# A fused dilated-attention and token/channel mixer kernel: a DMA transpose issued from ScalarE's queue, one block through another PSUM bank, two gate sums moved

## The chip, the cores and the metric

The kernel runs on one core of one Trainium2 chip. The metric is the time of one execution in device microseconds; the time before is the median of three runs. A profile of one further execution gives the span from the first to the last instruction, and every instruction's start and duration. TensorE has two rows in it: PE for the matmuls and PEld for the weight loads that overlap them. DVE is VectorE, ACT is ScalarE, POOL is GpSimd, SP is SyncE, which issues most DMAs here. A DMA that is issued from an engine's queue holds that queue while it is issued.

## The reference

Eight batches, eight heads, 576 positions of 64 numbers. Heads 0 to 3 see the last 32 positions, heads 4 to 7 every fourth of the last 128 (the dilated half). The attention's output x (576 x 512 for a batch) goes through a mixer:

```python
scores = (q @ k.T) / sqrt(64)                       # masked: plain window, or dilated
x = softmax(scores) @ v                             # heads side by side: (B, 576, 512)
h = relu(x.T @ w_tok1) @ w_tok2                     # token mixing, 576 -> 256 -> 576
u = x + h.T
out = u + relu(u @ w_ch1) @ w_ch2                   # channel mixing, 512 -> 1536 -> 512
```

## The kernel before

TensorE is given one long hand-made order. `interleave` takes a main sequence, `gen_main(b)` for batch b, and a list of steps with due times; it walks the main sequence, adds up costs that are written beside each piece, and puts a step in where the sum has reached its due time. The times are only numbers that set the order of the instructions; nothing is measured. Below, "block b" is what is issued while `gen_main(b)` runs. In it lie, for batch b, the channel mixing; for batch b+1, the attention's product with v (`values`), the token mixing (`emit_h1`, `emit_u`) and the turning of u; for batch b+2, the casts, the turning of q and k by DMA (`dma_steps`) and the scores with their exponentials (`scores_twin`); for batch b+3, the loads.

**The channel mixing.** `gen_main` makes twelve gate blocks of 128 channels (tile `gp`, L934; the last 64 rows of two batches together in tile `gt`, L925), and ScalarE writes relu of each into the SBUF tensor `gt` (L109). `gen_out` multiplies these by the second weights. It does the 2 x 2 block product with seven products in place of eight, so VectorE first makes sums of gate blocks (`gate_sums`, L737, four kinds named 1 to 4, each in two halves of 0.5 to 1 us) and, once, of weights. Products with the original weights and with `wsum_a`, `wsum_b` are summed in two PSUM banks, px (tile `yx`) and pw (tile `yw`); VectorE adds u and moves them to the SBUF tile `o` (`with_u`, L793; `with_t`, L798), and SP stores `o`. A bank is free for its next product when that add is done. In odd batches `tails` first multiplies the last 64 rows (tile `yp`, L747) and adds u to them (L752).

**u in three forms.** `emit_u` leaves u of a batch in the tile `u`, the dilated half (columns 256 to 511) with its rows sorted by their remainder by four, as attention gave it. The gate blocks need u transposed, the last add needs u with its rows in natural order. From batch 2 on this is done by DMA: SP transposes the whole of u into `utm` (L702) and, for odd batches, its last rows into `utt` (L700); ScalarE copies the dilated half of `utm` into `utd` with the rows in natural order (`uT_place`, L863, two copies); and `u_natural` transposes `utd` back onto the dilated half of u (L708, eight blocks of 128 x 128). There is one `utd`, so the next batch's two copies wait for that transpose, and so do the two `with_u` of the dilated half, (1, 1) and (0, 1). In the batches 0 and 1 TensorE makes the transposes, and VectorE copies them out of a PSUM bank (`emit_uT`).

**Scores to v.** For each half g of the heads, `scores_twin` lets TensorE fill six PSUM banks; ScalarE takes eight (g = 0) or six exponentials from them (L547), GpSimd multiplies the results by the masks (L115, tiles `attp`, `attd` and, for the last rows, `attt`), and only then can `values` of the next block run on TensorE. Heads 4 to 7 need `attd` and the second mask of `attt`.

**Queues and waits.** Each engine's queue runs in the order of issue, and a waiting instruction holds what is behind it. The DMAs that SP and ScalarE issue raise eight semaphores in turn (`DMAHW0` to `DMAHW7`); each waits first for the DMA before it on its own semaphore, so the name in that wait tells which one it raises. PSUM banks are taken in turn from rings: "main" (three banks), "sc" (two) and "fl" (three).

Of the kernel before, what the change touches and what calls it, by code (L numbers as in the profile page):

```python
# [9 lines left out]
FP16 = mybir.dt.float16  # L10
# [4 lines left out]
B = 8  # L15
# [53 lines left out]
def kernel(  # L69
# [11 lines left out]
    nc = tc.nc  # L81
# [583 lines left out]

    def emit_uT(b, cb):
        odd = b % 2
        p = bank("fl" if cb % 2 == (cb > 1 if b else 0) else "main", 3, f"tpu_{b}_{cb}", FP16)
        if odd:
            t = sb.tile([128, 640], FP16, tag="ut1", bufs=4, name=f"uT_{b}_{cb}")  # L670
        else:
            if b not in uT0:
                uT0[b] = sb.tile([128, 4, 512], FP16, tag="ut0", bufs=1, name=f"uT_{b}")
            t = uT0[b][:, cb]
        eng = nc.scalar if cb == 2 and not b else nc.vector
        m0 = 128 * odd
        if cb < 2:
            for s in range(4):
                nc.tensor.transpose(out=p[:, m0 + 128 * s:m0 + 128 * s + 128],
                                    in_=u16(b, s)[:, cb], identity=ident)  # L680
            if odd:
                nc.tensor.transpose(out=p[:, 0:128], in_=u16t[b // 2][:, cb], identity=ident)
            copy(eng, t, p[:, 0:512 + m0])
        else:
            grid = p[:, 0:4 * RS].rearrange("p (r i) -> p r i", i=RS)
            m0 = 32 * odd
            for s in range(4):
                nc.tensor.transpose(out=grid[:, s, m0:m0 + 128], in_=u16(b, s)[:, cb], identity=ident)
            if odd:
                nc.tensor.transpose(out=grid[:, :, 0:32], in_=u16t[b // 2][:, cb], identity=perm)  # L690
            copy(eng, natural(t), grid[:, :, 0:128 + m0].rearrange("p r m -> p m r"))
        uT[(b, cb)] = (t[:, 128:640], t[:, 0:128]) if odd else (t, None)
# [9 lines left out]
            nc.sync.dma_start_transpose(out=uTm[i].rearrange("p x s t -> p (x s) t"),  # L702
                                        in_=u16w[b].rearrange("p x s c -> p (x s c)"))

    def u_natural(b):
        u = u16w[b]
        if turned(b):
            nc.sync.dma_start_transpose(out=u[:, 2:4].rearrange("p x s c -> p (x s) c"),  # L708
                                        in_=uTd.rearrange("p x t -> p (x t)"))
            return  # L710
        for cb in (2, 3):
            nc.sync.dma_start_transpose(out=u[:, cb], in_=uT[(b, cb)][0])
# [26 lines left out]
    def gen_out(b):  # L739
# [16 lines left out]

        base = turn["main"]
        ahead = odd and not last
        gate_sums(b, 1, (2, 1, 4) if ahead else (2,))
        if odd and not last:  # L760
            tail = tails()
            yield next(tail)
            spare.append(base)
            yield from tail
        else:
            spare.append(base)
        turn["main"] = base + 2
# [145 lines left out]
    def gen_main(b):  # L913
        odd = b % 2
        order = CBS if b else range(4)
        m0 = 640 * odd

        def w3_block(cb, mb):
            return w3[mb // 4][:, cb, mb % 4:512:4]

        def gp_tails(g):
            p = bank("main", 3, f"gt_{b}_{g}")
            for i in range(4):
                for cb in order:
                    nc.tensor.matmul(  # L925
                        out=p[:, 128 * i:128 * i + 128], lhsT=w3_block(cb, 4 * g + i), rhs=uT[(b, cb)][1],
                        start=(cb == order[0]), stop=(cb == order[-1]))
            relu(nc.scalar, gta[:, 4 * g:4 * g + 4, 512:640],
                 p.rearrange("p (i t) -> p i t", t=128))

        for mb in range(NMB):
            p = bank("main", 3, f"gp_{b}_{mb}")
            for i, cb in enumerate(order):
                nc.tensor.matmul(out=p, lhsT=w3_block(cb, mb), rhs=uT[(b, cb)][0], start=(i == 0), stop=(i == 3))  # L934
                if i == 1:
                    yield 0.43
            relu(nc.vector if (mb in (1, 3, 5, 6) if b == 0 else mb in (1, 3, 5) if b == 1 else False) else nc.scalar, gta[:, mb, m0:m0 + 512], p)
            yield 0.43
            if odd and mb in (3, 6, 9):
                gp_tails(mb // 3 - 1)  # L940
                yield 0.9
            if b and mb == (6 if b == 1 else 10):
                for g in range(2):
                    gate_sums(b, g, (3,))
            if b and mb == (11 if b == 1 else 10):
                gate_sums(b, 0, (2, 1, 4) if odd and b + 1 < B else (2, 1))
        if b:
            yield from gen_out(b)
            return
        for i in (1, 2, 3):  # L950
            weight_sum(i)
        for s in range(4):
            if s == 2:
                weight_sum(4)
            p = bank("main", 3, f"yp_{b}_{s}")
            o32 = sb.tile([128, DM], FP32, tag="o32", bufs=4, name=f"o32_{b}_{s}")
            for half in range(2):
                c = slice(256 * half, 256 * half + 256)
                for mb in range(NMB):
                    a0 = s if half else 128 * s  # L960
                    nc.tensor.matmul(  # L961
                        out=p[:, c], lhsT=gta[:, mb, a0:512:4] if half else gta[:, mb, a0:a0 + 128],
                        rhs=w4[mb][:, c], start=(mb == 0), stop=(mb == NMB - 1))
                    if mb == 5:
                        yield 0.65
                if half:
                    nc.vector.tensor_tensor(out=blocks4(o32), in0=blocks4(p), in1=u16(b, s), op=ALU.add)
                    for i in range(2):
                        d = slice(256 * i, 256 * i + 256)
                        o = out[b, 0:512, d].rearrange("(m r) c -> r m c", r=4)[s] if i else \  # L970
                            out[b, 128 * s:128 * s + 128, d]
                        nc.sync.dma_start(out=o, in_=o32[:, d])
                yield 0.65
# [193 lines left out]
    for b in range(B):  # L1167
# [15 lines left out]
        elif b == 1:  # L1183
            steps += at(13.5, 0.0, [lambda: u_natural(1)])
            va = value_steps(2, 0.0, 1.0)
            steps += [(0.8 + 0.4 * i, c, f) for i, (_, c, f) in enumerate(scores2[10:])]
            steps += [(t, c, f) for t, (_, c, f) in zip((2.2, 3.0, 4.8, 5.6, 8.2, 9.0, 10.4, 11.2), va)]
            steps += mix_steps(2, 7.0, 13.0, 15.1, 24.6, 1.0, 5.6, 0.8)
            casts = cast_steps(3)
            steps += [(6.0 + 0.5 * i, 0.0, casts[i]) for i in (0, 2, 4, 6, 8)]  # L1190
            steps += [(9.5 + 1.0 * i, 0.0, lambda i=i: cast_qk(3, "q", i, nc.scalar)) for i in range(4)]
            steps += score_steps(3, 21.0, 9.5, lag=0.1)
            steps += at(20.8, 0.9, load_steps(4))
            loads, turns, places = [], dma_steps(3), place_steps(3)

            def some_v(lo, hi):
                if not loads:
                    loads.extend(load_v_steps(3))
                for f in loads[lo:hi]:
                    f()  # L1200

            steps += at(6.0, 0.0, [lambda: some_v(0, 4)]) + at(8.1, 0.0, [turns[0], turns[1], lambda: some_v(4, 7)])
            steps += at(10.6, 0.0, [turns[2], turns[3], lambda: some_v(7, 8)]) + at(12.6, 0.0, [turns[4]])
            steps += at(11.0, 0.3, casts[9:14]) + at(12.5, 0.0, [places[i] for i in (0, 1, 4)])
            steps += at(13.0, 0.3, casts[14:16]) + at(14.0, 0.0, places[2:4]) + at(14.2, 0.0, casts[16:])
        else:
            late = 2.4 * (b % 2)
            steps += at(14.6 + late / 6, 0.0, [lambda b=b: u_natural(b)])
            if b + 1 < B:
                va = value_steps(b + 1, 0.4, 0.95)  # L1210
                steps += va[:6] + [(t + late / 5, c, f) for t, c, f in va[6:]] + mix_steps(
                    b + 1, 5.4 + late / 6, 8.2 + late / 6, 10.6 + late / 6, 22.4 + late, 0.9, 4.1, 1.0)
            if b + 2 < B:
                steps += at(2.0, 0.6, cast_steps(b + 2)) + score_steps(b + 2, 21.4 if b % 2 else 18.0, 8.4 if b % 2 else 6.4)
                places = place_steps(b + 2)
                steps += at(8.5, 0.7, dma_steps(b + 2)) + at(12.0, 0.4, places[:4])
                steps += at(19.6 if b % 2 else 17.2, 0.0, places[4:])
            if b + 3 < B:
                steps += at(17.6, 0.9, load_steps(b + 3))
# [31 lines left out]
```

## Time and profile before

| | us |
|---|---|
| median of 3 runs (lowest to highest) | 278.54 (277.87 to 278.73) |
| the profiled execution, its own time | 278.42 |
| its span, first to last instruction | 276.6 |
| clock granted to TensorE, mean | 1.000 |
| VectorE busy | 168.3 |
| ScalarE busy | 149.0 |
| GpSimd busy | 158.8 |
| the busiest DMA queue (q1), share of the 16 engines in the span | 75.9% |

In a timeline each row has the start and the duration in us, the engine, the line, the operation with its output and inputs, and in square brackets how long the engine stood idle before it and what released it. SPq is SP's queue: its duration is the issue, not the transfer. The transfer's end is given as "DMA to landing", counted from the start of the issue.

### The profile page before, as it was taken

To read this page: it belongs to the slowest core of one execution; us is meant where nothing else is said; L and a number is where in the kernel's file an instruction comes from. 1 tells how busy PE (TensorE), PEld (TensorE's weight loads), DVE (VectorE), ACT (ScalarE), POOL (GpSimd) and SP (SyncE) were. 2 spreads that over 40 slices of the span, in tenths; PEclk is the share of its full clock that TensorE was granted. 3 is DMA by queue.
4 is the path that set the end of the run, shared out by engine and by line. 5 is a ranking of instruction groups with operands and counts; after the bars stand their busy time and mean duration, and the time that the engine had idled before them with its cause. 6 is when DMAs were issued, how large, how long until landed. Compare 5 with 4: busy or idle time off the path is not lost.

```text
span 276.6 us, 6790 instructions
## 1 busy us (share of the span) xinstructions
PE 265.8 (96%) x2694; PEld 197.2 (71%) x2694; DVE 168.3 (61%) x340; ACT 149.0 (54%) x291; POOL 158.8 (57%) x214
## 2 busy tenths in 40 slices
PE   6899999999999999997999999999999999999994
PEld 2796676897666876685775876687776866786673
DVE  6767668575568655674649454775475473961363
ACT  2864774363674465467545656476546565236500
POOL 7880760389858759849973589739980870000000
PEclk9999999999999999999999999999999999999999
DMA  7999999995979799999999999989999220553015
GB/s 216 271 248 238 291 241 210 316 241 159 343 132 226 151 316 281 233 165 259 304 221 186 257 280 255 172 156 316 304 211 148 81 79 2 99 147 78 0 40 152
DMA packets 116783, 55.50 MB, mean 201 GB/s; under 512 B 84976, under 2 KB 115696, under 8 KB 116752
## 3 DMA queue, kind: packets, MB, share of 16 engines
q1 hardware_dynamic: 112096, 49.63, 75.9%
q0 software_dynamic: 2640, 3.94, 7.9%
q10 hardware_dynamic: 2016, 1.51, 1.8%
q8 instruction: 21, 0.34, 0.5%
q14 instruction: 10, 0.08, 0.1%
HBM read 38.12 MB, written 9.44 MB: 172 GB/s over the span
## 4 chain that ended last, share of the span: by engine, by line
PE 85%; DMA 7%; DVE 4%; issue 1%; ACT 1%; ACTq 0%; POOL 0%; DVEq 0%
PE gp L934 29%; PE yx L778 12%; PE yw L778 9%; PE h1p L637 5%; PE up L649 4%; PE gt L925 4%; PE yp L961 4%; PE yp L747 3%; DMA lt<-in_k_dram 3%; PE sc L522 3%; DMA u<-utd 2%; DMA w1p<-in_moe_w_tok_dram 2%; PE h1p L635 1%; PE av L614 1%; PE av L619 1%; DVE gt L737 1%
## 5 line engine op out<-in xcount | busy, mean ns | idle before, releaser
L109 ACT ACTIVATE gt<-gp 128x512 f16<-128x512 f32 x89 | 53.2, 598 | 50.4 <-PE gp L934 50.1
L778 PEld LDWEIGHTS <-gt 128*128 128x128 f16 x600 | 57.0, 98 | 10.2 <-issue 2.0
L934 PE MATMUL gp<-utd,w 128*128 128x512 f16 x144 | 54.7, 380 | 0.0
L934 PE MATMUL gp<-utm,w 128*128 128x512 f16 x144 | 54.6, 379 | 0.0
L934 PEld LDWEIGHTS <-w 128*128 128x128 f16 x384 | 39.1, 113 | 19.8 <-issue 0.5
L115 POOL TENSOR_TENSOR attp<-attp,const 128x1280 f16<-128x1280 f16 x12 | 31.6, 2637 | 23.4 <-ACT attp L547 23.4
L737 DVE TENSOR_TENSOR gt<-gt 128x768 f16<-128x768 f16 x56 | 32.2, 605 | 12.5 <-ACT gt L109 12.2
L115 DVE TENSOR_TENSOR xn<-av,rec 128x320 f16<-128x320 f32 x64 | 31.4, 491 | 2.2
L115 POOL TENSOR_TENSOR attd<-attd,const 128x1024 f16<-128x1024 f16 x12 | 25.5, 2124 | 7.7 <-issue 5.4
L934 PE MATMUL gp<-uT,w 128*128 128x512 f16 x96 | 25.8, 380 | 0.0
L793 DVE TENSOR_TENSOR o<-yx,u 128x512 f32<-128x512 f32 x22 | 15.2, 689 | 11.2 <-PE yx L778 10.5
L778 PE MATMUL yx<-w,gt 128*128 128x256 f16 x168 | 20.6, 273 | 0.0
L778 PE MATMUL yx<-wsum_a,gt 128*128 128x256 f16 x168 | 20.6, 273 | 0.0
L547 ACT ACTIVATE attp<-sc 128x480 f16<-128x480 f32 (+1 forms) x36 | 15.9, 538 | 8.7 <-PE sc L522 8.7
L655 DVE TENSOR_TENSOR u<-up,xn 128x512 f16<-128x512 f32 x26 | 17.8, 688 | 4.1 <-PE up L649 4.1
L626 DVE RECIPROCAL rec<-av 128x5 f32<-128x5 f32 x64 | 12.2, 191 | 12.2 <-PE av L623 12.1
L105 POOL CAST c_k<-l_k 128x512 f16<-128x512 f32 x29 | 17.6, 616 | 2.2 <-DMA l_k<-in_k_dram 1.3
L863 ACT COPY utd<-utm 128x512 f16<-128x512 f16 x12 | 12.7, 1129 | 10.3 <-DMA u<-utd 6.6
L105 POOL CAST c_q<-l_q 128x512 f16<-128x512 f32 x26 | 16.3, 630 | 2.9 <-DMA l_q<-in_q_dram 2.2
L664 DVE TENSOR_TENSOR u16t<-up,xn 64x512 f16<-64x512 f32 x7 | 4.8, 689 | 21.0 <-PE up L660 21.0
L109 ACT ACTIVATE h<-h1p 128x256 f16<-128x256 f32 x31 | 11.8, 384 | 8.9 <-PE h1p L637 8.4
L798 DVE TENSOR_TENSOR o<-yw,o 128x512 f32<-128x512 f32 x13 | 9.0, 691 | 11.4 <-PE yw L778 11.3
(158 smaller groups left out, 549.6 us busy)
## 6 DMA issues: line engine op xcount, KB each, us to landing
l_q<-in_q_dram SPq DMA_DIRECT2D x15, 512.0 KB, 6.6
l_k<-in_k_dram SPq DMA_DIRECT2D x14, 512.0 KB, 7.4
out_dram<-o SPq DMA_DIRECT2D x26, 256.0 KB, 4.1
l_vn<-in_v_dram SPq DMA_DIRECT2D x32, 128.0 KB, 6.7
l_vd<-in_v_dram SPq DMA_DIRECT2D x16, 256.0 KB, 4.2
w<-in_moe_w_ch_dram POOLq DMA_DIRECT2D x6, 512.0 KB, 7.6
out_dram<-o SPq DMA_DIRECT2D x17, 128.0 KB, 2.7
l_vt<-in_v_dram SPq DMA_DIRECT2D x8, 256.0 KB, 4.7
```

Of the source, the lines that this page charges most:

```text
L105: eng.tensor_copy(out=out, in_=in_)
L109: nc.scalar.activation(out=out, in_=in_, func=AF.Relu)
L115: eng.tensor_tensor(out=out, in0=x, in1=y, op=ALU.mult)
L547: nc.scalar.activation(out=out, in_=in_, func=AF.Exp, scale=0.125)
L626: nc.vector.reciprocal(out=rec[:, :, 0], in_=av[:, :, 64])
L637: nc.tensor.matmul(out=p, lhsT=w[:, s, j], rhs=x[:, s, c], start=False, stop=(s == 3))
L655: nc.vector.tensor_tensor(out=u16(b, s), in0=blocks4(p), in1=blocks4(xn[b][:, s]), op=ALU.add)
L737: nc.vector.tensor_tensor(out=out, in0=x, in1=y, op=op)
L778: nc.tensor.matmul(out=p, lhsT=gta[:, k0 + mb, r:r + 128], rhs=weights[:, mb, c], start=(first and not mb and (not a or len(parts) > 2)), ...
L793: nc.vector.tensor_tensor(out=grid(o[(i, j)]), in0=grid(p), in1=u, op=ALU.add)
L863: nc.scalar.copy(out=natural(uTd[:, cb - 2]), in_=uTm[i][:, cb].rearrange("p r m -> p m r"))
L934: nc.tensor.matmul(out=p, lhsT=w3_block(cb, mb), rhs=uT[(b, cb)][0], start=(i == 0), stop=(i == 3))
```

## The change

Three edits. First, `emit_uT` takes one of batch 1's four blocks (cb = 1) through a bank of the ring "fl" in place of "main"; the output products of batch 0 use "main". Second, in odd blocks the gate sum 4 of the second half, and in block 1 that of the first half too, is issued behind the last rows' products and their add, no longer ahead. Third, for the batches 2 to 5 `u_natural` issues its transpose from ScalarE's queue, and at a later place (due time 17.3, or 19.7 in odd blocks, against 14.6 and 15.0); the batches 6 and 7 stay as they were.

```diff
     def emit_uT(b, cb):
-        p = bank("fl" if cb % 2 == (cb > 1 if b else 0) else "main", 3, f"tpu_{b}_{cb}", FP16)
+        p = bank("fl" if (cb != 2 if b else cb % 2 == 0) else "main", 3, f"tpu_{b}_{cb}", FP16)
...
-    def u_natural(b):
+    def u_natural(b, queue=nc.sync):
         u = u16w[b]
         if turned(b):
-            nc.sync.dma_start_transpose(out=u[:, 2:4].rearrange("p x s c -> p (x s) c"),
+            queue.dma_start_transpose(out=u[:, 2:4].rearrange("p x s c -> p (x s) c"),
                                         in_=uTd.rearrange("p x t -> p (x t)"))
...
-        gate_sums(b, 1, (2, 1, 4) if ahead else (2,))
+        gate_sums(b, 1, (2, 1) if ahead else (2,))
         if odd and not last:
             tail = tails()
             yield next(tail)
             spare.append(base)
             yield from tail
+            if b == 1:
+                gate_sums(b, 0, (4,))
+            gate_sums(b, 1, (4,))
...
-                gate_sums(b, 0, (2, 1, 4) if odd and b + 1 < B else (2, 1))
+                gate_sums(b, 0, (2, 1, 4) if odd and 1 < b < B - 1 else (2, 1))
...
-            steps += at(14.6 + late / 6, 0.0, [lambda b=b: u_natural(b)])
+            steps += at(14.6 + late / 6 if b + 2 >= B else 17.3 + late, 0.0,
+                        [lambda b=b: u_natural(b, nc.sync if b + 2 >= B else nc.scalar)])
```

SP's queue in block 2, before, with the waits of each row: the turning of k and q of batch 4 (`tt`, `kr`, `qt`), then `utm` of batch 3, u of batch 2, `utt` of batch 3, then loads.

```order
L353 DMA_TRANSPOSE qt<-c_q_1957 128x8x128 [waits DMAHW2_49]
L702 DMA_TRANSPOSE utm_90<-u_3_2104 128x16x128 [waits DMAHW3_49,DVE_49]
L708 DMA_TRANSPOSE u_2_1643<-utd 128x8x128 [waits DMAHW4_49,Activation_49]
L700 DMA_TRANSPOSE utt<-u16t_95 128x4x128 [waits DMAHW5_49]
L198 DMA lt_2176<-in_q_dram 64x8x64 [waits DMAHW6_49]
```

The same place of SP's queue with the change:

```order
L353 DMA_TRANSPOSE qt<-c_q_1957 128x8x128 [waits DMAHW2_49]
L702 DMA_TRANSPOSE utm_90<-u_3_2104 128x16x128 [waits DMAHW3_49,DVE_49]
L700 DMA_TRANSPOSE utt<-u16t_95 128x4x128 [waits DMAHW4_49]
L198 DMA lt_2176<-in_q_dram 64x8x64 [waits DMAHW6_49]
L198 DMA lt_2176<-in_k_dram 64x8x64 [waits DMAHW7_49]
```

The transpose of u has left SP's queue; `utm` raises semaphore 3, `utt` now 4, and 5 is that of the transpose that went to ScalarE.

ScalarE's queue in block 2, before: the last relu, a copy of k, and the exponentials of batch 4's first half.

```order
L109 ACTIVATE gt<-gp_11_2151 128x512 [waits PE_49]
L103 COPY kt<-kr 128x512 [waits DMAHW7_49,Pool_49]
L547 ACTIVATE attp<-sc_0_5_2193 128x2x128 [waits PE_49,Activation_49,Pool_49]
L547 ACTIVATE attt<-sc_0_5_2193 128x2x64 [waits Activation_49]
L547 ACTIVATE attp<-sc_0_0_2188 128x3x160 [waits Activation_49]
```

The same place with the change:

```order
L109 ACTIVATE gt<-gp_11_2150 128x512 [waits PE_49]
L103 COPY kt<-kr 128x512 [waits DMAHW7_49,Pool_49]
L708 DMA_TRANSPOSE u_2_1643<-utd 128x8x128 [waits DMAHW3_49,DMAHW4_49,DMAHW2_49,DMAHW5_49,DMAHW1_49,DMAHW6_49,DMAHW0_49,Activation_49]
L547 ACTIVATE attp<-sc_0_5_2193 128x2x128 [waits PE_49,Pool_49]
L547 ACTIVATE attt<-sc_0_5_2193 128x2x64
L547 ACTIVATE attp<-sc_0_0_2188 128x3x160
```

The transpose stands ahead of the eight exponentials, and it waits for seven of the DMA semaphores, among them 3 and 4, which `utm` and `utt` raise when they have landed. In the blocks 3, 4 and 5 it stands at the same place; in 3 and 5 there is no `utt`, and it waits for `utm`.

VectorE's queue in block 1, before: six gate sums ahead of the last rows' add (L752).

```order
L655 TENSOR_TENSOR u_2_1643<-up_3_1666,xn_1363 128x4x128
L737 TENSOR_TENSOR gt<-gt 128x3x256 x6
L752 TENSOR_TENSOR o_1_4_1740<-yp_4_1681,u16t_94 128x512
L793 TENSOR_TENSOR o_1_00_1760<-yx_1745,u_1_1040 128x512
L798 TENSOR_TENSOR o_1_00_1760<-yw_1762,o_1_00_1760 128x512
```

And with the change:

```order
L655 TENSOR_TENSOR u_2_1643<-up_3_1666,xn_1363 128x4x128
L737 TENSOR_TENSOR gt<-gt 128x3x256 x4
L752 TENSOR_TENSOR o_1_4_1738<-yp_4_1679,u16t_94 128x512
L737 TENSOR_TENSOR gt<-gt 128x3x256 x2
L796 TENSOR_TENSOR o_1_00_1760<-yx_1745,u_1_1040 128x512
```

Two of the six sums stand behind that add. TensorE's and GpSimd's orders of instructions are the same as before.

## The prediction

> **What bounds the kernel now.** I read the busy times first, then the list of waits, then the timeline of each engine where TensorE stood still.
>
> ```profile
> PE 265.8 (96%) x2694; PEld 197.2 (71%) x2694; DVE 168.3 (61%) x340; ACT 149.0 (54%) x291; POOL 158.8 (57%) x214
> ...
> ACT utd L863 <- DMA u<-utd: 6.6, 2, 4.2
> PE yw L778 <- DVE o L793: 1.5, 1, 1.5
> PE yp L961 <- DVE o L967: 0.4, 1, 0.4
> ```
>
> TensorE is busy for 96% of the span: the time is its work plus the gaps in its row. From 40 us on, its timeline shows only three of 0.2 us or more:
>
> ```profile
> 63.70 0.82 PE L961 MATMUL yp<-w,gt 128*128 128x256 f16 x6 [0.35 <-DVE o L967]
> 92.11 1.47 PE L778 MATMUL yw<-w,gt 128*128 128x256 f16 x12 [0.20 <-DVE o L752]
> 126.18 0.81 PE L778 MATMUL yw<-wsum_b,gt 128*128 128x256 f16 x6 [1.48 <-DVE o L793]
> ```
>
> These are the three places of the change: 0.35 + 0.20 + 1.48 = 2.03 us is all that it can win. What it can lose is not so bounded: TensorE's order is fixed, so any input that is late shifts everything behind it, to the end.
>
> **The two small edits.** At 63.70 TensorE waits for a "main" bank, since batch 1's cb = 1 block holds one turn of that ring; with that block in "fl" the bank before it is free. Worth 0.35 us at most. At 92.11 it waits for the last rows' add, which stood behind six gate sums; two of them behind it free the bank in time. Worth 0.20 us. Neither adds work. But both lie ahead of block 2, where below another chain decides, so I take them as absorbed: 0 of the possible 0.55 us.
>
> **The moved transpose, block 2.** Before, around the third gap:
>
> ```profile
> 117.89 1.09 ACT L103 COPY kt<-kr 128x512 f16<-128x512 f16 x1
> 120.16 0.38 ACT L547 ACTIVATE attp<-sc 128x256 f16<-128x256 f32 x1 [1.19 <-PE sc L522]
> ...
> 122.66 0.35 ACT L547 ACTIVATE attt<-sc 128x128 f16<-128x128 f32 x1
> ...
> 117.41 2.11 SPq L702 DMA_TRANSPOSE utm<-u  x1
> 119.61 1.69 SPq L708 DMA_TRANSPOSE u<-utd  x1
> 121.35 1.71 SPq L700 DMA_TRANSPOSE utt<-u16t  x1
> ...
> 125.44 0.69 DVE L793 TENSOR_TENSOR o<-yw,u 128x512 f32<-128x512 f32 x1 [2.16 <-DMA u<-utd]
> ```
>
> The times to landing of the three transposes, in the rows of each line (the six of L708 and of L702 together, then L702 and L700 here, then L702 in block 4):
>
> ```profile
> L708 SPq DMA_TRANSPOSE u<-utd x6: 1261/1554/1992, 119.6 to 249.0; - x6
> DMA to landing us min/median/max: 3.2/3.8/5.7
> ...
> L702 SPq DMA_TRANSPOSE utm<-u x6: 1317/2006/2934, 90.6 to 237.6; - x6
> DMA to landing us min/median/max: 4.3/4.6/6.3
> ...
> L702 SPq DMA_TRANSPOSE utm<-u x1: 2108/2108/2108, 117.4 to 117.4; - x1
> DMA to landing us min/median/max: 6.3/6.3/6.3
> ...
> L700 SPq DMA_TRANSPOSE utt<-u16t x1: 1714/1714/1714, 121.3 to 121.3; - x1
> DMA to landing us min/median/max: 4.6/4.6/4.6
> ...
> L702 SPq DMA_TRANSPOSE utm<-u x1: 1317/1317/1317, 177.8 to 177.8; - x1
> DMA to landing us min/median/max: 4.3/4.3/4.3
> ```
>
> So `utm` landed at 117.41 + 6.3 = 123.7, u at 119.61 + 5.7 = 125.3 (the longest of the six), `utt` at 121.35 + 4.6 = 125.95, 0.65 after u. The order of the changed program shows what takes their place. ScalarE comes to the transpose behind the copy of k, at 117.89 + 1.09 = 119.0; there it waits for the semaphores of `utm` and `utt` before it issues. `utm` is issued as before (what is ahead of it in SP's queue hasn't changed) and `utt` directly behind it, so I take `utt` landed at 123.7 + 0.65 = 124.35. ScalarE stands still for 5.35 us, then issues.
>
> No issue of a transpose from ScalarE is in the trace. The nearest rows are SP's: 1.26 to 1.99 us, median 1.55, which I take. ScalarE is free at 125.9. Behind it stand the eight exponentials, which took 122.66 + 0.35 - 120.16 = 2.85 us: they end at 128.75, not at 123.0. For these GpSimd waits, and TensorE for GpSimd:
>
> ```profile
> 122.98 2.76 POOL L115 TENSOR_TENSOR attp<-attp,const 128x1280 f16<-128x1280 f16 x1 [3.44 <-ACT attp L547]
> ...
> 129.56 2.12 POOL L115 TENSOR_TENSOR attd<-attd,const 128x1024 f16<-128x1024 f16 x1 [0.62 <-POOL attp L115]
> 131.65 1.15 POOL L115 TENSOR_TENSOR attt<-attt,const 128x512 f16<-128x512 f16 x1
> ...
> 134.02 0.28 PE L619 MATMUL av<-vv,attd 128*128 128x65 f16 x4
> ```
>
> The masks up to the second `attt` took 131.65 + 1.15 - 122.98 = 9.82 us with 0.62 idle among them, so 9.2 when they come late. They would end at 128.75 + 9.2 = 137.95; the product of head 4 with v, at 134.02, needs them. **Block 2 costs 137.95 - 134.02 = 3.95 us**, against a time before that has the gap of 1.48 in it already.
>
> The add of the third gap comes late too: u lands at 124.35 + 3.8 = 128.15, the add takes 0.69, TensorE's 126.18 becomes 128.9, or 2.7 us. That shift lies inside the 3.95. So the gap is not closed; it grows, and the masks then add to it.
>
> [...]
>
> **Block 4**, the same place with `utt`:
>
> ```profile
> 177.81 1.32 SPq L702 DMA_TRANSPOSE utm<-u  x1
> ...
> 181.59 0.38 ACT L547 ACTIVATE attp<-sc 128x256 f16<-128x256 f32 x1 [1.17 <-PE sc L522]
> ...
> 193.81 0.28 PE L619 MATMUL av<-vv,attd 128*128 128x65 f16 x4
> ```
>
> `utm` lands at 177.81 + 4.3 = 182.1, `utt` at 182.75; ScalarE is free at 184.3, the exponentials end at 187.15, the masks at 196.35 against 193.81: **2.55 us**. The add's shift (u lands at 186.55) is smaller again.
>
> **Blocks 3 and 5** have no `utt`, and last rows' products ahead of the scores.
>
> ```profile
> 147.95 2.25 SPq L702 DMA_TRANSPOSE utm<-u  x1
> ...
> 155.24 2.62 POOL L115 TENSOR_TENSOR attp<-attp,const 128x1280 f16<-128x1280 f16 x1 [5.27 <-ACT attp L547]
> ...
> 166.61 0.28 PE L619 MATMUL av<-vv,attd 128*128 128x65 f16 x4
> ```
>
> With the median landing `utm` is there at 152.55, ScalarE free at 154.1, the exponentials end at 156.95 (before: 155.24), the masks at 166.15, 0.45 us ahead of the 166.61 that needs them. Cost 0; the cover is those 0.45 us, and a `utm` that takes 6.3 us in place of 4.6 would cost 1.25. Block 5 is taken like block 3.
>
> SP wins four issues of about 1.55 us. It issues loads a little sooner; no gap of TensorE ends with a load there, so I count 0.
>
> **Sum.** Made against the profiled execution's own 278.42 us (0.12 under the median of the runs): 278.42 + 3.95 + 2.55 = 284.9. Nothing behind gives a shift back, as TensorE has no gap of 0.2 us after 126.18. Ends of the unknown terms: with an issue of 1.26 and the shortest `utm` (4.3), block 2 costs 3.95 - 0.3 - 2.0 = 1.65 and block 4 2.25; with 1.99 and, in block 4, the longest (6.3), 4.4 and 5.0. The small edits' 0.55 may come through whole.
>
> **The rivals.**
>
> 1. Quick landings: `utm` of block 2 takes 4.6, not 6.3, since nothing of u is in its way. Block 2 then costs 2.25 and the sum is 283.2; with the small edits coming through, 282.7, and at the low end 281.8. For it: 6.3 is the longest of six. Against: u was issued behind `utm`. Chance 0.2.
> 2. The odd blocks lose their cover of 0.45 us, each by 1.25: 287.4. For it: it takes only a late `utm`. Chance 0.13.
> 3. Faster: the wait on SP's transposes is met when ScalarE comes to it. Then the issue at 119.0 precedes the old 119.61, u lands at 122.8, and all three gaps close: 278.42 - 2.03 = 276.4. It decides if `utm` and `utt` have landed by 119.6. Against it: `utm` is issued only at 117.41 and the shortest landing of six is 4.3 us. Chance 0.06.
> 4. No change that a measurement of this kernel can tell (0.3%, 0.8 us): SP runs ahead of TensorE by so much that the wait costs what the small edits bring. Chance 0.03.
>
> **How the numbers follow.** The forecast, with its chance of 0.58, is 284.9 us. The range goes from 281.0, under the first rival's low end, to 288.0, over the second's sum; the third and fourth and what lies outside make up the rest. Slower: 0.58 + 0.2 + 0.13 = 0.91; within 0.3%: 0.03; faster: 0.06.
>
> **What would show it.** In the new profile: ScalarE's queue idle from about 119 to 124 in block 2 until `utm` or `utt` lands, then an issue of 1.3 to 2 us; the first `attp` mask of that block near 128.8; a gap of TensorE of 2.5 us or more at the add of (1, 1), and a further wait of `av` for the masks. In block 4 the same, smaller; in 3 and 5 none. The gaps at 63.70 and 92.11 gone. The prediction is wrong if ScalarE's exponentials start near 121, or if the masks are late and no `av` waits for them.

## The result, and the profile after

| | before | changed |
|---|---|---|
| median of 6 runs, us (lowest to highest) | 278.56 (277.61 to 278.73) | 298.21 (296.58 to 307.39) |
| ratio, 95% interval | | 1.0695, 1.0661 to 1.0729 |
| a profiled execution, its own time | 278.42 | 299.49 |
| its span | 276.6 | 297.7 |
| clock granted to TensorE, mean | 1.000 | 0.966 |

The change makes the kernel 7% slower: 19.65 us by the medians, against 6.5 forecast. Some executions of a kernel are disturbed and longer (here 306.77 and 307.39 us of the changed kernel's six): medians here and below are of all executions, ratios and intervals of the others alone. Every row of the changed kernel below is of a further execution, e1_changed_again, which lies 1.28 us over the median; the first profile, of the execution of 307.39 us, is used only where it is named.

The busy times and the longest waits of the changed kernel (us in total, times, the longest):

```profile
PE 271.8 (91%) x2694; PEld 200.4 (67%) x2694; DVE 169.0 (57%) x340; ACT 149.2 (50%) x291; POOL 156.5 (53%) x214
...
DVE o L796 <- DMA u<-utd: 15.9, 2, 10.1
PE yw L781 <- DVE o L796: 14.5, 2, 9.4
```

TensorE is idle for 26 us instead of 11, and two instructions hold 14.5 us of it: a product that waits for the add (L796, L793 before), which waits for the transpose of u. TensorE is also busy for 6.0 us more with the same 2694 matmuls. The timeline of TensorE has these gaps of over 0.6 us behind 40 us:

```profile
95.86 1.59 PE L781 MATMUL yx<-wsum_a,gt 128*128 128x256 f16 x12 [2.13 <-DVE o L796]
97.24 2.77 PE L781 MATMUL yw<-wsum_a,gt 128*128 128x256 f16 x12
...
138.21 1.44 PE L781 MATMUL yw<-wsum_b,gt 128*128 128x256 f16 x6 [9.40 <-DVE o L796]
...
204.73 1.44 PE L781 MATMUL yw<-wsum_b,gt 128*128 128x256 f16 x6 [5.13 <-DVE o L796]
```

One is in block 1, at the moved gate sums; two are at the add of (1, 1) in the blocks 2 and 4, the place forecast. Six products into `yw` that took 0.81 us before take 1.44, and twelve 2.77 in place of 1.47: the array runs at about half its rate. The stretches of TensorE at the second and third gap show the granted clock behind the busy times:

```profile
134.00:138.00 4.00, 0.00 (x0) 0.00 (x0) 0.54 (x1) 0.64 (x1) 4.00 (x3) 0.50 1.10 308
138.00:142.00 4.00, 3.79 (x39) 2.78 (x39) 0.90 (x3) 2.46 (x6) 0.00 (x1) 0.57 0.86 234
142.00:146.00 4.00, 4.00 (x47) 2.82 (x45) 2.88 (x8) 2.68 (x6) 3.28 (x3) 1.00 0.77 197
...
204.00:208.00 4.00, 3.27 (x34) 2.32 (x34) 1.37 (x2) 2.48 (x4) 2.28 (x1) 0.50 1.11 339
```

The columns are the stretch, its length, busy time of PE, PEld, DVE, ACT and POOL with counts, the clock, the DMA share and GB/s. In the blocks 2 and 4 the clock falls to 0.50 inside the gap and stays there for some us of work behind it.

ScalarE's and SP's queues in block 2 of the changed kernel, with the transposes as issues (ACTq, SPq):

```profile
121.99 1.11 ACT L103 COPY kt<-kr 128x512 f16<-128x512 f16 x1
127.79 1.52 ACTq L708 DMA_TRANSPOSE u<-utd  x1
129.41 0.38 ACT L547 ACTIVATE attp<-sc 128x256 f16<-128x256 f32 x1 [6.30 <-DMA lt<-in_q_dram]
...
120.49 1.86 SPq L702 DMA_TRANSPOSE utm<-u  x1
122.40 1.77 SPq L700 DMA_TRANSPOSE utt<-u16t  x1
124.22 2.08 SPq L198 DMA_DIRECT2D lt<-in_q_dram  x1
...
129.63 1.68 SPq L192 DMA_DIRECT2D l_k<-in_k_dram  x1
```

This is the mechanism as forecast: ScalarE stands from 123.1 until `utt` has landed, issues at 127.79, and the exponentials start behind that. The profile puts the wait down to `lt`; but the order shows `utt` among what ScalarE waits for, and the row of its line has it landed at 122.40 + 5.1 = 127.5, just ahead of the issue. What differs from the forecast is how long u then takes. The landing of `utt`, then the four transposes of ScalarE's queue, each in a stretch of its own, the blocks 2, 3, 4 and 5:

```profile
L700 SPq DMA_TRANSPOSE utt<-u16t x1: 1772/1772/1772, 122.4 to 122.4; - x1
DMA to landing us min/median/max: 5.1/5.1/5.1
...
L708 ACTq DMA_TRANSPOSE u<-utd x1: 1516/1516/1516, 127.8 to 127.8; - x1
DMA to landing us min/median/max: 9.6/9.6/9.6
...
L708 ACTq DMA_TRANSPOSE u<-utd x1: 1257/1257/1257, 163.7 to 163.7; - x1
DMA to landing us min/median/max: 6.8/6.8/6.8
...
L708 ACTq DMA_TRANSPOSE u<-utd x1: 1271/1271/1271, 196.3 to 196.3; - x1
DMA to landing us min/median/max: 7.6/7.6/7.6
...
L708 ACTq DMA_TRANSPOSE u<-utd x1: 1247/1247/1247, 231.8 to 231.8; - x1
DMA to landing us min/median/max: 3.1/3.1/3.1
```

Before, all six landed in 3.2 to 5.7 us. In the blocks 2, 3 and 4 SP issues batch b+3's loads at the same time (124.22 to 131.31 in block 2), and among them a store of `o` (127.76 in block 2); in block 5 there is no batch left to load.

Where the 21.1 us of the two spans lie, from the starts of the first matmul of the last rows of u in each block (L660):

| stretch | before | changed | difference |
|---|---|---|---|
| span's start to block 0's L660 | 50.77 | 51.79 | +1.02 |
| to block 1's | 31.48 | 30.97 | -0.51 |
| to block 2's (the moved gate sums) | 29.31 | 32.90 | +3.59 |
| to block 3's (block 2's transpose) | 29.89 | 39.26 | +9.37 |
| to block 4's (block 3's) | 31.54 | 31.54 | 0.00 |
| to block 5's (block 4's) | 28.24 | 35.84 | +7.60 |
| to block 6's (block 5's) | 31.54 | 31.54 | 0.00 |

The 1.02 lie ahead of everything that the change touches. The -0.51 holds the gap of 0.35 at 63.70, which is gone.

### The profile page after: what moved, and what is told of

Its sections match the earlier page's. It is cut to its first block, busy times and chain, and to the rows that moved or that the text cites. A ratio compares the mean times of both kernels' runs of the same rounds, so it can differ in the third digit from the quotient of the medians.

```text
span 305.6 us, 6794 instructions
## 1 busy us (share of the span) xinstructions
PE 274.9 (90%) x2694; PEld 201.5 (66%) x2694; DVE 170.6 (56%) x340; ACT 149.3 (49%) x291; POOL 157.0 (51%) x214
## 4 chain that ended last, share of the span: by engine, by line
PE 74%; DMA 13%; issue 4%; DVE 4%; POOL 1%; SPq 1%; ACTq 0%; ACT 0%; DVEq 0%; POOLq 0%
PE gp L937 24%; PE yx L781 11%; PE yw L781 8%; PE h1p L637 5%; PE up L649 4%; PE gt L928 4%; PE yp L964 3%; PE yp L747 3%; DMA l_vn<-in_v_dram 3%; DMA l_q<-in_q_dram 3%; PE sc L522 3%; DMA u<-utd 2%; DMA lt<-in_k_dram 2%; DMA l_vt<-in_v_dram 2%; DVE gt L737 2%
## 5 line engine op out<-in xcount | busy, mean ns | idle before, releaser
L781 PEld LDWEIGHTS <-gt 128*128 128x128 f16 x600 | 59.2, 101 | 27.3 <-issue 16.9
L737 DVE TENSOR_TENSOR gt<-gt 128x768 f16<-128x768 f16 x56 | 33.1, 617 | 13.8 <-ACT gt L109 13.5
L937 PE MATMUL gp<-uT,w 128*128 128x512 f16 x96 | 27.5, 400 | 0.0
L781 PE MATMUL yw<-wsum_b,gt 128*128 128x256 f16 x72 | 11.8, 312 | 14.2 <-DVE o L796 14.2
L781 PE MATMUL yx<-wsum_a,gt 128*128 128x256 f16 x168 | 21.6, 281 | 2.1 <-DVE o L796 2.1
L796 DVE TENSOR_TENSOR o<-yx,u 128x512 f32<-128x512 f32 x22 | 15.2, 690 | 12.5 <-PE yx L781 12.3
L781 PE MATMUL yx<-w,gt 128*128 128x256 f16 x168 | 21.7, 282 | 0.0
L866 ACT COPY utd<-utm 128x512 f16<-128x512 f16 x12 | 12.5, 1095 | 17.1 <-DMA u<-utd 13.4
```

The source lines that it names most:

```text
L737: nc.vector.tensor_tensor(out=out, in0=x, in1=y, op=op)
L781: nc.tensor.matmul(out=p, lhsT=gta[:, k0 + mb, r:r + 128], rhs=weights[:, mb, c], start=(first and not mb and (not a or len(parts) > 2)), ...
L796: nc.vector.tensor_tensor(out=grid(o[(i, j)]), in0=grid(p), in1=u, op=ALU.add)
L866: nc.scalar.copy(out=natural(uTd[:, cb - 2]), in_=uTm[i][:, cb].rearrange("p r m -> p m r"))
```

## The experiments

The theory: (a) u, issued from a queue of its own, lands late because SP's loads are in flight beside it; (b) the gaps lower the clock, which costs more behind them; (c) the gate sums are a loss of their own. The rivals: the place alone does it (u issued 3 us later, whatever the queue); the masks behind late exponentials do it; the clock alone explains what was not forecast.

**e1_changed_again**: the changed kernel as it is, for another profile.

> The changed kernel once more, for a second profile of it. If the cost sits in the blocks 2 and 4 and in the gate sums of block 1, TensorE has gaps of about 9, 5 and 2 us there, and u's transposes of the blocks 2 and 4 land 7 to 9 us after their issue on ScalarE; time near 298 us. If the first profile's gap of 5.8 us in front of an av product at 50.7 us (a late load of v) is part of the change's cost, it is here again; else it is gone.

299.49 us in its one execution. Its rows are those above. The late v is not part of the change's cost: the gap of 5.76 us in front of that product (50.70 in the first profile) is not here; the nearest, at 51.35, is one of 0.56 for a load of weights.

**e2_queue_alone**: the third edit alone, without the bank and the gate sums.

```diff
...
-            steps += at(14.6 + late / 6, 0.0, [lambda b=b: u_natural(b)])
+            steps += at(14.6 + late / 6 if b + 2 >= B else 17.3 + late, 0.0,
+                        [lambda b=b: u_natural(b, nc.sync if b + 2 >= B else nc.scalar)])
```

> The third edit alone: u's transpose of the batches 2 to 5 on ScalarE's queue at the late place; bank and gate sums as before. If this edit carries the cost, about 295 to 296 us, gaps in the blocks 2 and 4 as in the changed kernel (9 and 5 us) and none of 2 us in block 1. If the cost is spread over the three edits, 285 us or less. By the terms of the prediction it would be 284.9.

296.75 us against 278.73, ratio 1.0675 (1.0624 to 1.0726): 18.0 of the 19.65 us are this edit's. TensorE's timeline, with the `av` that needs the second masks, and GpSimd's second masks:

```profile
134.60 1.44 PE L778 MATMUL yw<-wsum_b,gt 128*128 128x256 f16 x6 [9.69 <-DVE o L793]
...
201.72 1.44 PE L778 MATMUL yw<-wsum_b,gt 128*128 128x256 f16 x6 [4.54 <-DVE o L793]
...
141.19 1.16 POOL L115 TENSOR_TENSOR attt<-attt,const 128x512 f16<-128x512 f16 x1
...
145.07 0.28 PE L619 MATMUL av<-vv,attd 128*128 128x65 f16 x4
```

By the same markers as in the table block 2 costs 152.50 - 111.77 - 29.89 = 10.84 us and block 4 218.52 - 184.04 - 28.24 = 6.24; the blocks 3 and 5 cost 0.00 and -0.01. In block 2, 9.69 - 1.48 = 8.21 are the gap and 2.63 come behind it. The masks that the forecast had as the last term were done at 142.35, 2.7 us ahead of their product: they do not set the time. That fells the rival of the masks for the size of block 2. The stretches around the gap:

```profile
128.00:130.00 2.00, 0.00 (x0) 0.00 (x0) 0.00 (x0) 2.00 (x6) 0.00 (x0) 1.00 1.08 346
130.00:132.00 2.00, 0.00 (x0) 0.00 (x0) 0.00 (x0) 0.84 (x3) 1.20 (x1) 0.51 1.18 264
...
138.00:140.00 2.00, 2.00 (x11) 1.40 (x10) 0.69 (x1) 1.96 (x4) 0.89 (x1) 0.50 0.58 132
```

The clock falls at about 130.0, 5 us into the gap, and comes back at about 140.2, 5.6 us behind its end. At half rate these 5.6 us do 2.8 us of work: about the 2.63. And while u is on its way (126.27 to 133.8) the DMA engines are full from 128 on (shares of 1.08 and 1.18 in the rows above).

**e3_bank_alone**: the bank's line alone.

```diff
-        p = bank("fl" if cb % 2 == (cb > 1 if b else 0) else "main", 3, f"tpu_{b}_{cb}", FP16)
+        p = bank("fl" if (cb != 2 if b else cb % 2 == 0) else "main", 3, f"tpu_{b}_{cb}", FP16)
```

> The first edit alone. By the prediction's reading: the gap of 0.35 us at 63.7 is gone and the time is 278.0 to 278.5 us, since block 2's wait for u's transpose (1.5 us before) takes most of it back. If the shift of the main ring of banks costs something further on, over 278.8 us.

278.87 against 278.73, ratio 1.0015 (0.9987 to 1.0043): nothing. The gap at 63.70 is gone, and block 2's has grown from 1.48:

```profile
126.97 0.49 PE L778 MATMUL yw<-wsum_b,gt 128*128 128x256 f16 x3 [1.84 <-DVE o L793]
```

By the markers of the table 0.51 us are won ahead of block 1's (30.97 for 31.48) and 0.51 lost in block 2 (30.40 for 29.89). What is won ahead of a chain of DMAs is given back where TensorE next waits for that chain, as forecast.

**e4_gate_sums_alone**: the second edit alone.

```diff
-        gate_sums(b, 1, (2, 1, 4) if ahead else (2,))
+        gate_sums(b, 1, (2, 1) if ahead else (2,))
...
             yield from tail
+            if b == 1:
+                gate_sums(b, 0, (4,))
+            gate_sums(b, 1, (4,))
...
-                gate_sums(b, 0, (2, 1, 4) if odd and b + 1 < B else (2, 1))
+                gate_sums(b, 0, (2, 1, 4) if odd and 1 < b < B - 1 else (2, 1))
```

> The second edit alone. By the prediction's reading the 0.20 us gap at 92.1 closes and the time is 278.3 to 278.6 us. If a gate sum of VectorE that runs while GpSimd multiplies a mask is held up by it (2.99 us in place of 0.55 in the first profile of the changed kernel), a gate sum behind the tails of block 1 takes 2 to 3 us, TensorE stands about 2 us in front of the second yx product there, and the time is 280 to 281 us.

280.30 against 278.73, ratio 1.0057 (1.0028 to 1.0086): a little slower, where the prediction had 0.20 us to win. VectorE's, GpSimd's and TensorE's timelines in block 1:

```profile
91.52 3.45 DVE L737 TENSOR_TENSOR gt<-gt 128x768 f16<-128x768 f16 x2
94.89 0.68 DVE L796 TENSOR_TENSOR o<-yx,u 128x512 f32<-128x512 f32 x1
...
91.95 2.60 POOL L115 TENSOR_TENSOR attp<-attp,const 128x1280 f16<-128x1280 f16 x1 [3.17 <-ACT attp L547]
...
95.62 1.87 PE L781 MATMUL yx<-wsum_a,gt 128*128 128x256 f16 x12 [2.13 <-DVE o L796]
```

The two sums (0.549 and 2.989 us by the rows of the line) took 3.45 us together; the second began at about 92.0, when GpSimd had just begun a mask of 2.60, and ended 0.4 us behind that. The add of (0, 0) stood behind it and held TensorE for 2.13 us, and the clock then halved for one stretch. That stretch does not come every time: 3.4 us at 0.5 take 0.006 off the mean clock, and six of the twelve executions, of 278.84 to 279.80 us, have a mean of 0.997 or more. The meeting is not of this run alone: in e1, and in the first profile of the changed kernel at 100.0 us, the second of the two sums also ended 0.4 us behind a mask of 2.60; in the first profile its row has 2.99 us. Why it takes 2.99 in place of 0.55 beside the mask is not shown.

**e5_queue_loads_late**: e2 with the loads of even blocks put off, so that block 2's u has no loads beside it.

```diff
-                steps += at(17.6, 0.9, load_steps(b + 3))
+                steps += at(17.6, 0.9, load_steps(b + 3)) if b % 2 else at(24.5, 0.5, load_steps(b + 3))
```

> The third edit alone, and in even blocks SP's loads for the batch b+3 are put behind the store that needs u's transpose, so that none of them is under way while ScalarE's transpose is. If the loads on SP's queue stretch that transpose (7.5 us to landing in block 2, 5.4 in block 4 of the third edit alone), it lands in 3.1 to 3.6 us, the gaps of 9.7 and 4.5 us in TensorE's row fall to about 5.5 and 2, and the time to 284 to 289 us, unless the late loads cost something themselves (the next run tells). If the transpose is slow because it comes from ScalarE's queue, it still takes over 5 us and the gaps stay.

293.26 against 279.19, ratio 1.0452 (1.0358 to 1.0545). The landings of block 2's and block 3's u:

```profile
L708 ACTq DMA_TRANSPOSE u<-utd x1: 1352/1352/1352, 125.0 to 125.0; - x1
DMA to landing us min/median/max: 3.2/3.2/3.2
...
L708 ACTq DMA_TRANSPOSE u<-utd x1: 1258/1258/1258, 158.2 to 158.2; - x1
DMA to landing us min/median/max: 8.6/8.6/8.6
```

SP's first load and TensorE's gaps in its timelines:

```profile
130.24 0.69 SPq L198 DMA_DIRECT2D lt<-in_q_dram  x1
...
129.04 1.44 PE L778 MATMUL yw<-wsum_b,gt 128*128 128x256 f16 x6 [4.51 <-DVE o L793]
...
167.59 1.44 PE L778 MATMUL yw<-wsum_b,gt 128*128 128x256 f16 x6 [4.45 <-DVE o L793]
```

With the loads behind it (the first at 130.24), u lands in 3.2 us where e2 had 7.5 (the DMA view of its block), from the same queue and place. SP's store of `o` is gone from beside it too: it is issued at 121.49, where e2 issued it at 125.95. TensorE goes on at 129.04, where the forecast had 128.9. The block costs 145.66 - 111.20 - 29.89 = 4.57 us. That this lies near the forecast's 3.95 is luck: 4.51 - 1.48 = 3.03 of it are the gap, and 1.54 come behind it, where the clock is 0.50 until about 131.9; the 3.95 were for the masks, and at the products that need them TensorE has no gap here.

In block 4, too, no load is issued beside u, only a store of 256 KB:

```profile
194.20 0.39 SPq L806 DMA_DIRECT2D out_dram<-o  x1
...
L708 ACTq DMA_TRANSPOSE u<-utd x1: 1292/1292/1292, 194.1 to 194.1; - x1
DMA to landing us min/median/max: 5.4/5.4/5.4
```

u takes 5.4 us there, where e2's took 7.0 (not the 5.4 of the expectation) with store and loads, and the gap is 3.00 us for 4.54. So the loads are not all of it: here u is late without them. Whether the store does it is not shown: two stores of 128 KB, issued just ahead of u in block 5 (227.96 and 228.54), leave it at 3.2 us, and from 197 to 198 the DMA engines move only 16 GB/s with u still on its way. In block 3 u has loads beside it in both runs and takes 8.6 us (issued among loads at 156.15 to 161.37) and 7.0 in e2; the gap of 4.45, which e2 doesn't have, comes mostly from the issue, 12.5 us behind the block's marker for 8.8. As a cure the late loads are poor: the kernel stays 4.5% slower than before, and the 284 to 289 us expected were missed.

**e6_before_loads_late**: the same loads put off in the kernel before, u on SP, as a control.

```diff
-                steps += at(17.6, 0.9, load_steps(b + 3))
+                steps += at(17.6, 0.9, load_steps(b + 3)) if b % 2 else at(24.5, 0.5, load_steps(b + 3))
```

> The kernel before with the same late loads: what they cost alone. 278 to 281 us if the loads have the slack; more if the casts of the next block wait for them. u's transpose is issued from SP as before and the gap of 1.5 us in block 2 stays or shrinks.

287.58 against 279.19, ratio 1.0261 (1.0171 to 1.035), a ratio from three executions: a loss that was not expected. Its profile has it in one place, ahead of the block in which u is first turned by DMA:

```profile
51.99 0.21 PE L623 MATMUL av<-vt,attt 128*128 128x65 f16 x1 [6.65 <-POOL vt L105]
```

From block 2 on it runs as the kernel before (29.85 us for 29.89 in block 2). So the late loads cost block 2 nothing, and u, with no loads behind it, takes 5.6 us there, about the 5.7 of before: in SP's own queue the loads behind u had not made it slower. Why v comes late at 52 us was not settled, nor that the late loads do it: e5 has the same loads and reaches block 0's marker at 50.77 us like the kernel before, and the first profile of the changed kernel had its 5.76 us at the same product without them. So e5's time as a whole can't be set against e2's; its block 2 can.

**e7_late_place_on_sp**: the later place of the change, but on SP's queue; in block 2 u stands behind `utt` and ahead of the loads.

```diff
-            steps += at(14.6 + late / 6, 0.0, [lambda b=b: u_natural(b)])
+            steps += at(14.6 + late / 6 if b + 2 >= B else 17.3 + late, 0.0, [lambda b=b: u_natural(b)])
```

> The late place alone: u's transpose of the batches 2 to 5 at the due time of the change, but still issued from SP, directly behind utt or utm. If the place is what costs, 290 us or more. If the queue is, SP issues it 1.7 us later than before in the even blocks, it lands near 126 in block 2, the gap there is about 2 us in place of 1.5, and the time 278.5 to 280 us.

281.58 against 279.19, ratio 1.0029 (0.9979 to 1.0079): no difference that can be told. Block 2's u by the rows of its line:

```profile
L708 SPq DMA_TRANSPOSE u<-utd x1: 1258/1258/1258, 124.5 to 124.5; - x1
DMA to landing us min/median/max: 3.1/3.1/3.1
```

TensorE's timeline there:

```profile
128.41 0.82 PE L778 MATMUL yw<-wsum_b,gt 128*128 128x256 f16 x6 [3.33 <-DVE o L793]
```

The place alone widens the gap to 3.33 us (in an execution of 282.28 us); the queue makes it 9.7. That is more than the 2 us expected, since SP came to `utm` at 119.86, 2.4 us later than before (e2: 119.31). Issued from SP with the loads behind it, u lands in 3.1 us even though they follow 1.3 us later; in block 3, where three loads stand ahead of it, it takes 5.3. The time, 0.3% over that of before, fells the rival of the place.

**e8_early_on_sp**: u earlier on SP's queue (due 8.4), with the bank's edit.

```diff
-            steps += at(14.6 + late / 6, 0.0, [lambda b=b: u_natural(b)])
+            steps += at(8.4, 0.0, [lambda b=b: u_natural(b)])
```

> Another way to the same aim: u's transpose of the batches 2 to 7 issued from SP ahead of the turning of k and q (due time 8.4), with the first edit (bank). utd has been ready since the block before, so it lands some 8 us ahead of its use. If the gap of 1.5 us in block 2 is the only place where it was late, that gap and the one of 0.35 us close: 276.5 to 277.3 us. If it pushes k, q and utm back on SP's queue by 1.3 us each time and these are late then, 278.5 us or more.

277.78 against 279.19, ratio 0.9952 (0.9915 to 0.9988): a little faster. Block 2's gap is gone, but u now stands ahead of the turned q, and TensorE waits 0.50 us for `qt` at 119.44. In the blocks 2 to 5 u is issued directly behind the loads and stores of the block before and takes 4.4, 7.1, 6.1 and 4.3 us, from SP's own queue: it is not ScalarE's queue as such that makes u slow.

**e9_gaps_filled**: e2 with products of a tile of zeros added to px at the add's wait, 40 in block 2 and 18 in block 4, so that TensorE is not idle there. They are extra work, not part of the reference.

```diff
+            for _ in range({2: 40, 4: 18}.get(b, 0)):
+                nc.tensor.matmul(out=px, lhsT=idle[:, 0:128], rhs=idle, start=False, stop=True, skip_group_check=True)
```

> The third edit alone, with 40 (block 2) and 18 (block 4) matmuls on zeros put where TensorE stands waiting for u; they add 0 to the bank px, so nothing of the result is changed, and take 8.6 and 3.9 us of the 9.7 and 4.5 us gaps at the full clock. If the gaps cost more than their own length because the granted clock falls to 0.5 during them (for 10.2 us in block 2 and 3.4 in block 4 of the third edit alone), the clock stays at 1.00, the stretch from the end of the gap to the first up product of the last rows takes 15.3 us again in both blocks in place of 17.9 and 16.8, and the time falls by 3 to 4 us against the third edit alone (296.75). If the masks behind the late exponentials are what fills these stretches, they stay and so does the time.

295.46 against 278.74, ratio 1.0605 (1.0578 to 1.0632). The mean clock of its runs is 0.994, where e2's is 0.971 to 0.977; the time is 1.3 us under e2's. Inconclusive for the size of the clock's part: the clock is held, but less comes back than the 2.63 and 6.24 - 4.54 = 1.70 us that e2 lost behind its gaps, and without a profile of a usual execution (the one taken was of 482.09 us) it is open whether the fills ran past the add or something else was late by then. It shows that the clock is not the main part of the 18 us.

**e10_one_sum_moved**: of the second edit only gate sum 4 of the second half, which does not meet the mask.

```diff
-        gate_sums(b, 1, (2, 1, 4) if ahead else (2,))
+        gate_sums(b, 1, (2, 1) if ahead else (2,))
...
             yield from tail
+            gate_sums(b, 1, (4,))
```

> The second edit with one gate sum behind the tails in block 1, not two. If the 2.99 us of the second sum come from its meeting GpSimd's mask (both started at 100.0 us in the first profile), one sum ends before the mask starts, no sum there takes over 0.7 us, no gap of 2.1 us in block 1, time 278.3 to 278.9 us. If sums behind the tails are slow in themselves, the one is too, and the time is 279.5 us or more.

279.23 against 278.74, ratio 1.0017 (0.998 to 1.0054). VectorE and GpSimd:

```profile
91.59 0.55 DVE L737 TENSOR_TENSOR gt<-gt 128x768 f16<-128x768 f16 x1
...
91.93 2.67 POOL L115 TENSOR_TENSOR attp<-attp,const 128x1280 f16<-128x1280 f16 x1 [1.85 <-ACT attp L547]
```

The sum that is under way when the mask starts takes its 0.55 us, and block 1 has no gap. One sum costs nothing that can be told; the second, which starts after the mask, is the loss.

**e11_u_ahead_of_utm**: e10, the bank's edit, and u on SP directly ahead of `utm`.

```diff
-            steps += at(14.6 + late / 6, 0.0, [lambda b=b: u_natural(b)])
+            steps += at(11.4, 0.0, [lambda b=b: u_natural(b)])
```

> u's transpose of the batches 2 to 7 from SP directly ahead of utm (due time 11.4), the first edit, and one gate sum behind the tails. u lands about 121 us in block 2, 2 us ahead of its use; utm is issued 1.7 us later and lands before ScalarE's copies need it. If the three gaps of the kernel before close and no wait takes their place, 276.4 to 277.0 us; if utm's delay shows, a wait of the gate blocks for utd's copies and 277.5 us or more.

277.76 against 278.74, ratio 0.9971 (0.9934 to 1.0007). SP's timeline in block 2:

```profile
116.61 1.29 SPq L708 DMA_TRANSPOSE u<-utd  x1
117.98 2.31 SPq L702 DMA_TRANSPOSE utm<-u  x1
```

All six of u land in 3.1 to 4.8 us. In its profile TensorE has no gap of 0.12 us or more behind 38 us, and the span, 274.7 us, is 1.9 under that of before, whose three gaps held 2.03. But the runs scatter, and the interval just takes in no change. e8's interval does not; both beat the changed kernel by 7%.

## Why the prediction was wrong

The side was right (slower), and so were the first link, ScalarE's stand, and the places; the size was not, nor the term that was to set it: 284.9 forecast, 298.21 measured, outside the range. By steps:

- **The stand of ScalarE: right.** It waits for `utm` and `utt` and then issues. Counted from block 2's marker (4.10 us later than before), the changed kernel issued at 127.79 - 4.10 = 123.7, forecast 124.35; in block 4 (13.47 later) at 182.8, forecast 182.75. The issue, unseen before and taken as 1.55, measured 1.25 to 1.62.
- **"u lands at 124.35 + 3.8": the step that failed.** The median of six landings from SP's queue was carried to ScalarE's. There u had been issued ahead of the loads in one queue; from its own it flies beside them: 9.6 and 7.6 us in the blocks 2 and 4. Already the 5.7 us of the same block's row, in place of the 3.8, would have made the add's shift 4.6 us, more than the masks' 3.95. Put into the forecast's sum for the add, 2.7 + (9.6 - 3.8) - 0.65 = 7.85 us: measured, 9.40 - 1.48 = 7.92. In e2 u took 7.5, but SP had come to `utm` late and ScalarE issued 1.7 us behind the forecast (126.27, the block 0.21 late): 2.7 + 3.7 + 1.7 = 8.1, measured 8.21. For block 4 u lands at 196.30 + 7.6 = 203.9, and TensorE goes on at 204.73. e5 shows the cause in block 2: with neither loads nor a store beside it, the same transpose takes 3.2 us from the same queue, and the forecast's 128.9 is met to 0.14 us (to 0.5 counted from the block's marker, which is 0.36 early there). e7 has 3.1 from SP's queue with the loads behind it. In block 4 the loads are a part only: without them it still took 5.4 us (e5).
- **"The masks then add to it": right in their time, wrong as the bound.** With u on time (e5) they ended at 137.12 + 1.17 = 138.29, forecast 137.95. In e2 they had 2.7 us to spare, because the add's shift was longer than theirs. In e1, e2 and e5 no `av` of the blocks 2 and 4 stands 0.2 us or more for them; late masks that no `av` waits for were one of the prediction's own signs of being wrong. (Its two differences are 3.93 and 2.54 us, not 3.95 and 2.55, which changes nothing.)
- **TensorE's clock: left out.** The sum took the work behind a gap at its old rate. The rest of the blocks' cost is of this kind: 9.37 - 7.92 = 1.45 us in block 2 and 7.60 - 5.13 = 2.47 in block 4. In e1 the clock comes back at about 141.4 and 209.7, 3.2 and 5.0 us behind the ends of the gaps; at half rate that is 1.6 and 2.5 us of work. e9 shows that it is not the main part.
- **The gate sums "behind it free the bank in time; worth 0.20 us": wrong.** The step looked at VectorE's queue alone, not at what GpSimd does when the sum is put there. Measured: 3.59 us lost in block 1 of the changed kernel, 1.6 by e4's medians. That the 0.20 us could be won is not shown: with one sum moved (e10) the gap at 92.11 is gone, but so it is in the profiles of e3, e5 and e7, which keep all six sums ahead.
- **The bank "absorbed": right** (e3). **The odd blocks at 0: right**, although u was late there too (6.8 us in block 3). **SP's four saved issues at 0: wrong in what it overlooked**: the loads move up to where `u` stood, which is what u then meets.
- **The third rival, a wait that is met when ScalarE comes to it: wrong.** The wait of the program's order cost ScalarE 4.7 us in block 2 (123.1 to 127.8). Why the program has that wait is not shown.

The parts add up within their intervals: by the ratios e2, e3 and e4 give 6.75 + 0.15 + 0.57 = 7.47% for the 6.95% of all three edits. What stays open: the clock's exact share (e9), what besides the loads holds u in block 4 (e5), why block 2's u took 9.6 us in the changed kernel and 7.5 in e2, and e6's late v.

## What to carry to other kernels

Here one and the same transpose took 3.1 to 9.6 us to landing, with the queue the same and other transfers around it, so a landing time was no property of the instruction: when a DMA is moved to another queue, look up which transfers stood behind it, since these now run beside it. A DMA put on the queue of an engine that computes brings its waits with it, and everything behind it on that engine waits too: here 4.7 us in block 2, with eight exponentials behind it. When an operation is moved to a time of its own engine, look at what the other engines start at that moment; and price a gap of TensorE like those measured here, of 2.13 to 9.69 us, with the slow clock that came in or behind them, 3.4 to 10.2 us at 0.5.

## What the runs showed of the hardware

- **The clock.** Behind 40 us it fell to 0.5 in or just behind the gaps of TensorE of 2.13 us and more in the profiles of e1, e2 and e4 to e7, for stretches of about 3.4, 6.8 or 10.2 us: 3.4 at 2.13 (e4), at 3.33 (e7) and at e2's 4.54, 6.8 at 5.13 (e1), 10.2 at 9.69 (e2). The gaps of 1.48 (before) and 1.84 (e3) had no such stretch. The kernel before stood for 2.54 us ahead of its first matmul with a clock of 1.00 all through.
- **A transpose of eight 128 x 128 blocks within SBUF** lands 3.1 to 3.2 us after its issue where no load is issued beside it in block 5 (e1, e2, e5) and block 2 (e5), but 5.4 in e5's block 4, beside a store of 256 KB. In SP's own queue it takes 3.1 to 6.0 ahead of loads (before, e4, e7's block 2, e11) and 4.3 to 7.1 among or behind loads and stores (e7's block 3, e8's blocks 2 to 5); from ScalarE's queue 6.8 to 9.6 beside loads (e1, e2, e5). How the DMA engines share their time among the queues is not shown by any run here.
- **A gate sum of 128 x 768 on VectorE** took 0.54 to 1.46 us in the kernel before (median 0.55 of 56), and 2.99 when it began with or just behind the start of a mask of 2.60 us on GpSimd (e4, the first profile of the changed kernel).
